# Products of zeros moved into the bank of the weights' sums of squares, each sum made in one run, and a new table of order (block-sparse attention and an MLP, one core of Trainium2)

## The chip, the cores and the metric

The kernel runs on one core of one Trainium2 chip. The metric is the device time of a run in microseconds (us). Below, PE is TensorE, DVE is VectorE, ACT is ScalarE, POOL is GpSimd, and SP is the engine whose queue issues almost all transfers. The kernel before took 716.0 us in the median of 3 runs (714.64 to 716.82).

## The reference, cut to what matters

```python
# batch 4, 8 heads, 768 positions, head dimension 64; blocks of 32 positions, 24 blocks
scores = scale * np.matmul(q, k.transpose(0, 1, 3, 2))
mask = np.abs(blk_i - blk_j) <= 1
mask = mask | (blk_i == 0) | (blk_j == 0) | (blk_i == n_blocks - 1) | (blk_j == n_blocks - 1)
for qb in range(n_blocks):
    for kb in sampled_blocks[qb]:            # 3 random blocks for each block of queries
        mask[qb*32:(qb+1)*32, kb*32:(kb+1)*32] = True
attn = softmax(np.where(mask, scores, -1e9))
x = np.matmul(attn, v)                       # laid out as 3072 tokens x 512
h = x @ w_in                                 # 512 x 2048
g = h * np.tanh(np.log1p(np.exp(h)))
out = g @ w_out                              # 2048 x 512
```

## The kernel before, in words

The work has two halves that share the engines. **Attention** is cut into 52 jobs, 13 for each of the 4 batches (b = 0 to 3, jobs 0 to 12 for b = 0). A job takes two blocks of queries with their sampled keys, or one dense block (the first and the last of a batch). Its steps are the scores on PE (names `s_`, lines 767 for b = 0 and 777 for the others), the maxima on DVE (`mx_`, lines 815 to 820), the exponentials on ACT (`pt_`, line 846), for b = 0 the transposes on PE (`t_`, line 866) with their copies (`pp_`), the products with v on PE (`o_`, lines 931 and 947), the division and the turning of the result on DVE (`xs_`, `tx_`), and its two 16-bit parts (`xh_`, `xl_`). The keys and values of the sampled blocks are gathered by copies on POOL or ACT (`kg`, lines 691 and 693) and by transfers (`vg`, lines 721 to 727).

**The MLP** works on 12 tiles of 256 tokens. Each tile is 16 halves of h (12 matmuls of 128x256 each, line 1206) and 16 pieces of y (6 matmuls of 128x512 each, line 1267). The text calls a half of h or a piece of y a *unit*; there are 384 of them, and they are emitted in a fixed order among themselves. A tile of h needs the outputs of four or five attention jobs. Between h and y, ACT, DVE and POOL form g (`hs`, `us`, `g`, lines 1215 to 1253).

**The weights** arrive as 64-bit numbers and are decoded on DVE by three instructions for each piece (`add_decode`, lines 1059, 1062 and 1065): 8 pieces of w_in (`wr_0` to `wr_7`) and 16 pieces of w_out (`wor_0` to `wor_15`). The sum of squares of the decoded weights gives a power of two as scale: PE multiplies the pieces with themselves into one tile (`gram`, line 468), DVE takes the diagonal of it (line 483), PE adds it up over the partitions (`tp_`), and DVE halves the exponent (`root`, `scales_w`, `scale_o`). w_in has four such scales, each over two pieces, and w_out has one over all 16. Only behind the scale can the weights be split into two 16-bit parts (`wi hi`, `wi lo`, `wo t`, `wo hi`, `wo lo`), which h and y need.

**Products of zeros.** While PE has nothing to do in the first 150 us of the plan, the planner inserts matmuls of a zero tile (line 1038) that nobody reads; they keep PE active. They write into a tile of their own in PSUM: one of the two buffers of ring "h", which are the buffers of h. It is given back when job 9 has begun (`LAST = 9`). So h has one buffer until then.

**What sets the order.** Nothing is issued at once: each step is a task with a planned duration, the engines that can do it, what it reads and writes, and a key from the table `PRIO` (a number for each name and batch). `Plan.emit` then runs a model of the engines forward, always takes the task that can start first (ties by ready time plus key), and emits it. The chip's engines execute in that order, each its own queue, and wait for each other by semaphores. `START` holds planned earliest dates of the first scores, and `RES` a reserve of MLP work. Of the lines that the change touches, these set the shape of the sums of squares:

```python
for n, k in enumerate(keys):
    add("PE", ..., lambda n=n: fn(n), r=[k], w=[kg], new=[(ring, kg)] if n == 0 else (), ...)
```

Each piece of a sum of squares is thus a task of its own, which may stand among other work.

Of the kernel before, what the change touches and what calls it, by code (L numbers as in the profile page):

```python
# [31 lines left out]
    "zrow": (372.5, 343.3, 692.1, -386.3),  # L32
    "zeros": (-1154,),
    "load32 k": (-526.4,),
    "load32 q": (-410.3, -316, 360.9),
    "load v": (-388.9, -306.9, -105.1, -271.1),
    "which": (374.7,),
    "globals": (320.9, 485.3, -720.3, -426.6),
# [18 lines left out]
    "s": (-864, 750.5, -137, 427.9),
    "mx": (410.2, -131.2, 200.2, -747.1),
    "nb": (-606.3, -537, 242),
    "ex": (217.2, -56.8, -191.8, -287.8),  # L60
    "t": (-303.3, 16),
    "pp": (-297.6,),
    "o": (556.5, 15.4, 219, -227.1),
    "xs": (268.3, -141.9, -24.2, -148.8),
    "tx": (-680, -469.1, -691.3, -304.2),
    "xh": (55.5, 554.4, 66.8, 979.6),
    "xl": (-667.3, -368.2, -452.3, -1192),
    "gather k": (622.3, 656.4, 976.5, 1107),
    "gather v": (219.6, 175.4, 18.2, 365.6, -161, 297.2, -517.1, -299.6, -190.2, 611.6, 639.4, 218.3, -570.5,
        -60.5, 269, 108.9, -152.2, 257.3, -154, -170.8, -439.7, -662.4, -12, -183.7, -50.1, 330.5),  # L70
    "load wo": (5.1, 39.8, -463.1, 534.1),
    "decode wor": (-599.6, 24.8, -199.8, -61.5),
    "gram wo": (-838.3,),
    "diag wo": (-562.7,),
    "rootp wo": (178.5,),
    "root wo": (-306.6,),
    "wo t": (-705.8, -195.4, -913.6, -705.3),
    "wo hi": (-316.9, -351.8, -693.9, -792.3),
    "wo lo": (210.8, -523.1, -6.2, 7.7),
    "load k": (59, 59, 59, 134.3),  # L80
    "ss k": (70, 70, 70, 253.6),
    "sc k": (4, 1508, 439.1, 797.7),
    "rootp k": (60, -763.3, 391, -473.3),
    "root k": (7, -270.1, 54.7, -564.5),
    "hi k": (52, -142.1, -699.7, -237.7),
    "lo k": (-79, -88.8, 241.5, 528.5),
    "load q": (59, 59, 59, 665),
    "ss q": (70, 70, 70, -337.7),
    "rootp q": (60, -231.2, -546.9, -273),
    "root q": (7, -533.3, 127.1, -138.6),  # L90
    "hi q": (52, -297.2, -83.6, -744),
    "lo q": (-79, 39.7, -29.6, -293.5),
    "clear": (-985.4,),
    "dense v": (334.4, -79.2, 92.1, -172.8),
    "sc v": (4, 170.2, 343.1, 342),
# [1395 lines left out]
```

## Time and profile before

| what | value |
|---|---|
| median of 3 runs | 716.0 us (714.64 to 716.82) |
| time of the profiled execution | 717.17 us |
| its span in the trace | 715.4 us |
| PE busy | 679.7 us (95%) |
| DVE busy | 579.3 us (81%) |
| ACT busy | 530.6 us (74%) |
| POOL busy | 259.6 us (36%) |

The span is the time from the first to the last event of the trace; what lies around it is 1.8 us. PE counts as busy also while it multiplies zeros or runs at a lower clock, so the share alone does not tell how much of the MLP is done. The first 160 us differ from the rest: there the weights are decoded and PE has less work than time.

### The profile page before, as it was taken

What the parts mean: (1) busy time and instruction counts of PE and PEld (TensorE: products, weight loads), DVE (VectorE), ACT (ScalarE), POOL (GpSimd) and SP (SyncE); (2) the same over time, 40 slices, a digit from 0 to 9 for tenths busy, and PEclk for the clock granted to TensorE, in tenths of its full rate; (3) what the DMA queues carried; (4) which work ended last, traced back from release to release, by engine and by line L of the source; (5) the groups of instructions that cost most, each with busy time, mean ns of one, the idle gap of its engine ahead of it and who ended that gap; (6) DMA issues with size and microseconds to landing.
All of it is one profiled execution on the core that took longest, in us unless ns stands there. A gap on an engine that the chain in (4) does not pass through costs nothing.

```text
span 715.4 us, 25363 instructions
## 1 busy us (share of the span) xinstructions
PE 679.7 (95%) x10349; PEld 451.6 (63%) x10349; DVE 579.3 (81%) x1083; ACT 530.6 (74%) x874; POOL 259.6 (36%) x326
## 2 busy tenths in 40 slices
PE   8877889899999999999999999999999999999997
PEld 3544467666666666666666666666666666666653
DVE  4899999999979977989988978989979868454350
ACT  4845649989888967879878887978798758655440
POOL 3545634874344421544534203533524223000000
PEclk9998999999999999999999999999999999999999
DMA  9978893464785995695656575866655566520000
GB/s 333 383 220 252 269 299 97 124 166 99 173 169 131 199 212 131 163 255 148 143 146 191 137 206 137 245 189 132 162 132 131 134 133 158 131 76 16 16 16 29
DMA packets 144600, 115.94 MB, mean 162 GB/s; under 512 B 96739, under 2 KB 107492, under 8 KB 144484
## 3 DMA queue, kind: packets, MB, share of 16 engines
q1 hardware_dynamic: 144480, 114.33, 60.8%
q8 instruction: 81, 1.33, 0.8%
q14 instruction: 35, 0.29, 0.1%
q10 hardware_dynamic: 4, 0.00, 0.0%
HBM read 79.32 MB, written 12.95 MB: 129 GB/s over the span
## 4 chain that ended last, share of the span: by engine, by line
PE 55%; DVE 25%; ACT 7%; DMA 6%; issue 4%; SPq 1%; POOL 1%; ACTq 0%; POOLq 0%; DVEq 0%
PE y L1267 25%; PE h L1206 22%; PE o L947 3%; PE s L777 3%; DVE mx L820 3%; DMA vg<-vd 2%; ACT pt L846 2%; DVE p L897 2%; DVE wi L1065 2%; DMA wr<-in_moe_w_in_dram 1%; DVE wi L1062 1%; DVE tx L1001 1%; DVE hs L1240 1%; DVE nb L835 1%; DVE xs L978 1%
## 5 line engine op out<-in xcount | busy, mean ns | idle before, releaser
L1206 PE MATMUL h<-xh,wi 128*128 128x256 f16 x1536 | 283.1, 273 | 0.0
L1267 PE MATMUL y<-wo,g 128*128 128x512 f16 x1152 | 277.6, 379 | 1.0 <-ACT ys L1278 0.5
L1206 PEld LDWEIGHTS <-wi 128*128 128x128 f16 x2304 | 222.4, 98 | 58.7 <-issue 4.6
L1206 PE MATMUL h<-xl,wi 128*128 128x256 f16 x768 | 209.8, 273 | 0.0
L1267 PEld LDWEIGHTS <-g 128*128 128x128 f16 x1152 | 109.0, 98 | 104.8 <-issue 5.6
L846 ACT ACTIVATE pt<-s,nb,ns 128x256 f32<-128x256 f32 (+1 forms) x208 | 106.4, 577 | 8.2 <-DVE nb L835 7.3
L691 POOL COPY kg<-kt 128x256 f16 (+1 forms) x147 | 77.3, 564 | 75.0 <-PE s L777 54.8
L1215 ACT ACTIVATE hs<-h 128x512 f32<-128x512 f32 x96 | 56.7, 590 | 60.0 <-PE h L1206 59.8
L1240 DVE SCALAR_TENSOR_TENSOR hs<-us,hs 128x1024 f32<-128x1024 f32 x48 | 64.2, 1337 | 28.0 <-ACT us L1239 28.0
L1021 POOL CAST xh<-tx 128x256 f16<-128x256 f32 (+1 forms) x40 | 28.7, 726 | 121.2 <-DVE tx L1001 120.4
L897 DVE SCALAR_TENSOR_TENSOR p<-pt,p 128x512 f16<-128x512 f32 (+1 forms) x102 | 63.6, 643 | 0.8 <-ACT p L890 0.4
L1230 ACT ACTIVATE us<-hs,hsc 128x1024 f32<-128x1024 f32 x48 | 55.2, 1150 | 1.1
L1234 DVE TENSOR_SCALAR us<-us 128x1024 f32<-128x1024 f32 x48 | 34.1, 711 | 26.8 <-ACT us L1230 26.4
L820 DVE TENSOR_REDUCE mx<-s 128x4 f32<-128x1024 f32 x44 | 53.3, 1212 | 3.0 <-PE s L777 2.2
L1251 POOL TENSOR_TENSOR g<-hs,g 128x1024 f16<-128x1024 f32 x18 | 42.4, 2353 | 34.8 <-DVE g L1248 26.0
L1024 POOL TENSOR_TENSOR xl<-tx,xh 128x256 f16<-128x256 f32 (+1 forms) x45 | 37.5, 838 | 41.7 <-ACT xh L1019 25.8
L1238 ACT ACTIVATE us<-us 128x1024 f32<-128x1024 f32 x48 | 50.7, 1057 | 2.3 <-POOL us L1236 1.3
L1237 ACT ACTIVATE us<-us 128x1024 f32<-128x1024 f32 x38 | 40.1, 1055 | 15.7 <-DVE us L1234 15.6
L1239 ACT ACTIVATE us<-us 128x1024 f32<-128x1024 f32 x48 | 50.7, 1057 | 0.8
L693 ACT ACTIVATE kg<-kt 128x256 f16 (+1 forms) x117 | 36.7, 379 | 13.5 <-DMA kt<-in_k_dram 5.4
L947 PEld LDWEIGHTS <-pp 128*32 128x32 f16 x2952 | 32.5, 97 | 11.9 <-issue 11.4
L1253 DVE TENSOR_TENSOR g<-hs,g 128x1024 f16<-128x1024 f32 x30 | 37.4, 1248 | 2.0 <-ACT g L1246 1.6
(205 smaller groups left out, 914.8 us busy)
## 6 DMA issues: line engine op xcount, KB each, us to landing
vg<-vd SPq DMA_DIRECT2D x304, 65.0 KB, 2.4
vg<-vd SPq DMA_DIRECT2D x80, 195.0 KB, 3.1
wr<-in_moe_w_in_dram SPq DMA_DIRECT2D x8, 1024.0 KB, 10.6
wor<-in_moe_w_out_dram SPq DMA_DIRECT2D x16, 512.0 KB, 6.4
vd<-v SPq DMA_DIRECT2D x12, 520.0 KB, 5.7
raw_v<-in_v_dram SPq DMA_DIRECT2D x12, 512.0 KB, 4.9
out_dram<-ys SPq DMA_DIRECT2D x24, 256.0 KB, 2.4
raw_q<-in_q_dram SPq DMA_DIRECT2D x9, 512.0 KB, 4.8
```

Source lines behind the costliest of these rows:

```text
L691: nc.gpsimd.tensor_copy(out=dst, in_=src)
L820: nc.vector.tensor_reduce(out=mx.rearrange("p g w -> p (g w)"), in_=tl[ks].rearrange("p g (w k) -> p (g w) k", k=KT), axis=AX.X, op=ALU.max)
L846: ex = lambda o, x, g, w: nc.scalar.activation(out=o, in_=x, func=AF.Exp, bias=nb[:, g, w:w + 1], scale=ns(w)[:, 0:1])
L897: nc.vector.scalar_tensor_tensor(out=x[:, 1, cs], in0=src, scalar=PSC, in1=x[:, 0, cs], op0=ALU.mult, op1=ALU.subtract)
L947: nc.tensor.matmul(o[cs, at] if v1 == VW else o[cs, at, 0:v1 - v0], p[:, k, g, cs], x, start=j == 0 and g == 0 and k == 0 and n == 0, stop ...
L1206: nc.tensor.matmul(h[:, f2].rearrange("p (s q) -> p s q", q=BS), wi[:, fp, w, cc, fs], x[:, :, cc], start=f2 == 0 and k == 0, stop=f2 == 1 ...
L1215: nc.scalar.activation(out=tl[kq][:, 2 * (fp % 2):2 * (fp % 2) + 2], in_=tl[kh], func=AF.Copy, scale=-2.0 * GSC)
L1230: nc.scalar.activation(out=us(), in_=hs(), func=AF.Exp, scale=hsc[:, b, k:k + 1])
L1238: add("ACT", 0.97, lambda: nc.scalar.activation(out=us(), in_=us(), func=AF.Ln, bias=1.0), w=[ku], key=K("ln", b))
L1239: add("ACT", 0.97, lambda: nc.scalar.activation(out=us(), in_=us(), func=AF.Exp, scale=-1.0), w=[ku], key=K("un", b))
L1240: add("DVE", 1.15, lambda: nc.vector.scalar_tensor_tensor(out=hs(), in0=us(), scalar=-0.5, in1=hs(), op0=ALU.add, op1=ALU.mult), r=[ku], w ...
L1267: nc.tensor.matmul(tl[ky], tl["g", b, t, k][:, g, f, q], wo[:, fc, w], start=fc == 0 and n == 0, stop=fc == NFC - 1 and n == 2)
```

## The change

Three things change in the code, and a fourth follows from them.

1. The tile into which the products of zeros write is no longer a buffer of h. It is the one buffer of ring "y" (`("yz",)`), which y does not need before w_out is split. It is held until the diagonal of w_out is taken. h has both of its buffers from the start.
2. The sums of squares use the first 128 columns of that same tile, and the products of zeros the other 384, so a product of zeros is 128x384 and no longer 128x512.
3. A sum of squares is one task on PE, which needs all of its pieces: 16 matmuls in a row for two pieces of w_in, 64 in a row for the 16 pieces of w_out.
4. `PRIO`, `START` and `RES` are new in nearly all their numbers, and with them the order of the whole program. The number of products of zeros goes from 119 to 165. The other matmuls keep their number.

```diff
-        for n, k in enumerate(keys):
-            add("PE", 0.8 if key[0] == "wi" else 0.45, lambda n=n: fn(n), r=[k], w=[kg], new=[(ring, kg)] if n == 0 else (),
-                key=K(name, n0), lat=0.25)
+        add("PE", (0.55 if key[0] == "wi" else 0.36) * len(keys), lambda: [fn(n) for n in range(len(keys))],
+            r=[*keys, *([("iv", n) for n in range(NQ)] if key[0] == "wo" else [])], w=[kg], new=[("gy", kg)], use=[("yz",)],
+            key=K(name, n0), lat=0.25)
...
-        add("DVE", 0.4, diag, r=[kg], w=w, new=new_, key=K("diag " + key[0], n0))
+        add("DVE", 0.4, diag, r=[kg], w=w, new=new_, use=[("yz",)], key=K("diag " + key[0], n0))
...
-            nc.tensor.matmul(spare[0].rearrange("p (n q) -> p n q", q=P), z16, z16.unsqueeze(1).to_broadcast([P, 4, P]),
+            nc.tensor.matmul(spare[0][:, P:].rearrange("p (n q) -> p n q", q=P), z16, z16.unsqueeze(1).to_broadcast([P, 3, P]),
...
-    LAST = 9
-    add("PE", 0.0, lambda: spare.append(new(ps["h"], "h", ("zeros",), [P, 512])), w=["zeros"], new=[("h", ("zeros",))],
+    add("PE", 0.0, lambda: spare.append(new(ps["y"], "y", ("yz",), [P, 512])), w=["zeros"], new=[("y", ("yz",))],
...
-        if i == LAST:
-            add("PE", 0.0, spare.clear, r=["zeros", ("begun", i)], use=[("zeros",)], key=K("clear", 0))
...
+            add("PE", 0.0, spare.clear, r=["zeros", ("am", "wo")], use=[("yz",)], key=K("clear", 0))
...
-    RES, START = 949.9, [53.9, 10.3, 0, 62.9, 42.9, 3.5, 60.8, 74.5, 31.2, 92.3, 3.1, 0, 64.4, 30.3, 104.4, 183, 166.3, 159.2]
+    RES, START = 2252, [35.4, 4.3, 15.7, 18.9, 0, 0, 82, 52, 7.4, 64.2, 85.4, 7, 109.7, 96.5, 102.7, 32.5, 161.8, 120]
```

Where the order changes, three places are shown.

**DVE, at the maxima of jobs 8 and 9.** Of before, the rows ahead of the maxima of job 8 (`mx_8`); `wor_7` and `wor_13` are pieces of w_out, and the third instruction of their decoding is L1065:

```order
L1062 SCALAR_TENSOR_TENSOR wo_74<-wor_13_1604,wo_74 128x512
L1065 SCALAR_TENSOR_TENSOR wo_74<-wor_7_1435,wo_74 128x512
L1065 SCALAR_TENSOR_TENSOR wo_74<-wor_13_1604,wo_74 128x512
L968 TENSOR_SCALAR r_5_1719<-o_5_1484,iv_r_117 128x4
L972 RECIPROCAL r_5_1719<-r_5_1719 128x4
L983 TENSOR_TENSOR xs_5_1722<-o_5_1484,r_5_1719 128x256
L820 TENSOR_REDUCE mx_8_1735<-s_8_1538 128x4
```

Of the change, the rows around the maxima of job 9 (`mx_9`), on the same engine:

```order
L1065 SCALAR_TENSOR_TENSOR wo_74<-wor_3_1380,wo_74 128x512
L1059 TENSOR_SCALAR wo_74<-wor_14_1606 128x512
L1065 SCALAR_TENSOR_TENSOR wo_74<-wor_11_931,wo_74 128x512
L1062 SCALAR_TENSOR_TENSOR wo_74<-wor_14_1606,wo_74 128x512
L820 TENSOR_REDUCE mx_9_1749<-s_9_1659 128x4
L1065 SCALAR_TENSOR_TENSOR wo_74<-wor_14_1606,wo_74 128x512
L968 TENSOR_SCALAR r_5_1783<-o_5_1576,iv_r_117 128x4
```

Before, 14 of the 16 pieces of w_out are decoded ahead of the maxima of job 8; now it is 5 of 16, and 10 of 16 ahead of the maxima of job 9. Jobs 8 and 9 stand ahead of decoding that they stood behind.

**DVE, at the end of the decoding of w_out, in the change.** `wor_7` is the last piece, `am_wo` the diagonal of the sum of squares of w_out, and `hs_0_0_0` and `g_0_0_0` belong to the first tile of the MLP:

```order
L1065 SCALAR_TENSOR_TENSOR wo_74<-wor_7_1747,wo_74 128x512
L1001 STREAM_TRANSPOSE tx_6_1981<-xs_6_1962 128x256
L1240 SCALAR_TENSOR_TENSOR hs_0_0_0_1695<-us_0_0_0_1846,hs_0_0_0_1695 128x1024
L1234 TENSOR_SCALAR us_0_0_1_1979<-us_0_0_1_1979 128x1024
L1253 TENSOR_TENSOR g_0_0_0_2055<-hs_0_0_0_1695,g_0_0_0_2055 128x1024
L1240 SCALAR_TENSOR_TENSOR hs_0_0_1_1901<-us_0_0_1_1979,hs_0_0_1_1901 128x1024
L483 SCALAR_TENSOR_TENSOR yz_123,am_wo_2106<-yz_123,ident_64 128x128
```

Before, the diagonal of w_out stands behind the last piece with one such product of the MLP between them (the maxima of job 9 and the first part of one g besides); now two groups of h are that far ahead of it.

**PE, at the end of the run of w_out, in the change.** The last of the 64 matmuls into `yz_123` stand between the two halves of `h_0_0_4`, the fifth group of h of the first tile:

```order
L468 MATMUL yz_123<-wo_74 128x128
L931 MATMUL o_7_2063<-vg0_114,pp_7_0_1635 32x65 x16
L1206 LDWEIGHTS wi_73
L1206 MATMUL h_0_0_4_1965<-xh_0_0_599,wi_73 128x256
L1206 LDWEIGHTS wi_73
L1206 MATMUL h_0_0_4_1965<-xl_0_0_600,wi_73 128x256
```

Of before, a piece of the same sum (`gram_wo_1389`), which stands between the two halves of the first group of h; 11 more pieces follow, among h, scores and products with v:

```order
L1206 MATMUL h_0_0_0_1624<-xh_0_0_560,wi_73 128x256
L468 LDWEIGHTS wo_74
L468 MATMUL gram_wo_1389<-wo_74 128x128
L468 LDWEIGHTS wo_74
L468 MATMUL gram_wo_1389<-wo_74 128x128
```

So nine units of h stand ahead of the run, and the run ahead of everything else. When PE comes to the scores of job 13 (`s_13`, the first of batch 1), it has 32 units behind it in the change (26 halves of h and 6 pieces of y), and 27 before (22 and 5). The attention steps ahead of `s_13` on PE are the same in both.

## Rows read from the trace of the kernel before

**Rows 1.** Busy time by stretch: us, then PE, PEld, DVE, ACT, POOL, clock.

```profile
core 0: us, PE busy (x) PEld busy (x) DVE busy (x) ACT busy (x) POOL busy (x), PEclk, DMA share, GB/s
...
80.00:100.00 20.00, 16.44 (x228) 10.76 (x228) 18.44 (x37) 10.23 (x17) 7.59 (x8) 0.91 0.91 300
...
120.00:150.00 30.00, 28.12 (x532) 20.50 (x531) 29.49 (x47) 29.78 (x44) 25.25 (x27) 0.94 0.48 126
...
200.00:300.00 100.00, 98.62 (x1584) 66.58 (x1583) 87.31 (x183) 80.96 (x135) 39.54 (x47) 1.00 0.72 169
```

**Rows 2.** PE in order of time: start, us, work.

```profile
89.76 0.28 PE L1206 MATMUL h<-xh,wi 128*128 128x256 f16 x1
...
98.60 0.63 PE L468 MATMUL gram_wo<-wo 128*128 128x128 bf16 x8 [1.16 <-DVE wo L1065]
...
107.31 0.60 PE L866 MATMUL t<-ident,pt 128*128 128x128 f32 x4
...
110.86 0.39 PE L468 MATMUL gram_wo<-wo 128*128 128x128 bf16 x4
...
150.83 0.66 PE L931 MATMUL o<-vg,pp 128*32 128x65 f32 x32
...
159.06 1.17 PE L777 MATMUL s<-kt,q 64*32 64x512 f16 x48
```

**Rows 3.** The chain that ended last: one half of h, one piece of y.

```profile
161.63 1.31 PE h L1206 x12
...
173.60 1.30 PE y L1267 x6
```

**Rows 4.** DVE in order of time, at five places.

```profile
57.23 3.04 DVE L1065 SCALAR_TENSOR_TENSOR wi<-wr,wi 128x1024 int32<-128x1024 int32 x1
...
61.73 0.27 DVE L483 SCALAR_TENSOR_TENSOR gram_wi<-gram_wi,ident 128x128 f32<-128x128 f32 x1
...
107.72 1.47 DVE L1065 SCALAR_TENSOR_TENSOR wo<-wor,wo 128x512 int32<-128x512 int32 x2
...
110.25 1.21 DVE L820 TENSOR_REDUCE mx<-s 128x4 f32<-128x1024 f32 x1
...
160.99 1.21 DVE L815 TENSOR_REDUCE mx<-s 128x2 f32<-128x1024 f32 x1
```

**Rows 5.** Groups by line and shape: count, busy us, mean ns.

```profile
L1240 DVE SCALAR_TENSOR_TENSOR hs<-us,hs 128x1024 f32<-128x1024 f32 x48 | 64.2, 1337 | 28.0 <-ACT us L1239 28.0
...
L1065 DVE SCALAR_TENSOR_TENSOR wo<-wor,wo 128x512 int32<-128x512 int32 x16 | 11.0, 703 | 0.0
...
L1062 DVE SCALAR_TENSOR_TENSOR wo<-wor,wo 128x512 int32<-128x512 int32 x16 | 12.2, 770 | 0.0
...
L1059 DVE TENSOR_SCALAR wo<-wor 128x512 int32<-128x512 int32 x16 | 8.3, 532 | 1.3 <-DMA wor<-in_moe_w_out_dram 1.3
...
L1253 DVE TENSOR_TENSOR g<-hs,g 128x1024 f16<-128x1024 f32 x30 | 37.4, 1248 | 2.0 <-ACT g L1246 1.6
...
L1248 DVE CAST g<-hs 128x1024 f16<-128x1024 f32 x30 | 21.1, 704 | 9.1 <-PE y L1267 8.8
...
L1024 DVE TENSOR_TENSOR xl<-tx,xh 128x128 f16<-128x128 f32 x5 | 3.5, 726 | 0.0
...
L879 DVE COPY pp<-t 128x512 f32<-128x512 f32 x10 | 6.8, 676 | 1.2 <-PE t L866 1.2
...
L835 DVE TENSOR_SCALAR nb<-mx,ns 128x4 f32<-128x4 f32 x16 | 9.4, 588 | 0.1
...
L1230 ACT ACTIVATE us<-hs,hsc 128x1024 f32<-128x1024 f32 x48 | 55.2, 1150 | 1.1
...
L693 ACT ACTIVATE kg<-kt 128x256 f16 x87 | 29.6, 407 | 2.3 <-PE s L777 1.3 <-POOL kg L691 0.5 <-DVE us L1234 0.3
```

**Rows 6.** PE and its clock while h already ran.

```profile
101.00:104.00 3.00, 3.00 (x47) 0.50 1.10 349
...
138.50:141.50 3.00, 2.92 (x42) 0.50 0.24 62
```

More of the change, by code (lines that the diff above doesn't have):

```diff
@@ L27 @@
              xs=1, hs=3, us=3, g=4, ys=1, kt=1, q=2, ssk=2, ssv=2, ssq=2, sck=2, scv=2, scq=2, iv=2, ns=3, ws=2,
-             wq=2, am=2, p16=3, tx=1)
+             wq=2, am=2, gy=1, p16=3, tx=1)
 PRIO = {
[L32 to L38, printed above, removed]
[16 rows of a table removed]
-    "gsc": (-69.1,),
-    "open": (163,),
@@ L57 @@
[L57 to L95, printed above, removed]
-    "ends": (13, 542.7, 466.1, 1080),
-    "hi v": (52, -74.3, 62.8, 85.1),
@@ L111 @@
-    "un": (184.5, 575.9, -457.3, -178.2),
-    "hm": (-41.7, 485.8, 146.2, 619.7),
-    "gh": (91.4, 381.2, 177, -262.4),
-    "gl": (259.1, 389.1, 749.5, 495.9),
-    "ys": (-27.1, -7.7, -30.1, -83.4),
-    "out": (-436.7, -87.9, 351.5, -286.7),
+    "zrow": (35.9, 246.1, 437.6, -570.6),
+    "zeros": (-488.9,),
+    "load32 k": (-802.2,),
+    "load32 q": (-960.9, -534.7, 391.8),
+    "load v": (-780, -345.7, -304.5, 138.6),
+    "which": (466.7,),
+    "globals": (142.5, -437.7, -1403, -1272),
[16 rows of a table added]
@@ new lines @@
+    "gsc": (300.2,),
+    "open": (389.4,),
+    "s": (-293.5, 1022, 204.8, 611.3),
+    "mx": (660.3, -204.8, 662.9, -265.1),
+    "nb": (-619.9, -926.8, -586, 120.7),
+    "ex": (990.9, -35, -144.6, -626.4),
+    "t": (-84.8, 16),
+    "pp": (-432.7,),
+    "o": (165.9, -309.5, 166.2, -1448),
+    "xs": (423.7, -118.7, 436.6, -211.1),
+    "tx": (-1314, -228.9, -1034, -842.6),
+    "xh": (336.7, 776.3, -829.3, 987),
+    "xl": (-360, 272, -807.1, -1820),
+    "gather k": (1627, 1242, 1408, 1924),
@@ new lines @@
+    "gather v": (-99.1, 229.5, -365.9, 124.5, -1214, 89.8, -418.7, -635.6, -870.5, 52.6, 605.1, -399.6, -812.7,
+        -990.2, -232.3, -274.4, 114.7, 465.5, 322.4, -311.2, -865.1, -1403, -12, 41.5, -164.9, -935.3),
+    "load wo": (-794.8, 65.7, -849.6, -124.7),
+    "decode wor": (110.5, 349.6, 151.2, 6.4),
+    "gram wo": (-630.1,),
+    "diag wo": (-474.9,),
+    "rootp wo": (814,),
+    "root wo": (76.4,),
+    "wo t": (-666.7, -198.5, -869.3, -544.1),
+    "wo hi": (-500.6, -568.5, -2019, -1351),
@@ new lines @@
+    "wo lo": (907.4, 209, -229.4, 528),
+    "load k": (59, 59, 59, 109.7),
+    "ss k": (70, 70, 70, 502.5),
+    "sc k": (4, 1966, 411.7, 478.6),
+    "rootp k": (60, -467.2, 366.9, 94.8),
+    "root k": (7, -600.5, -43.8, 76.4),
+    "hi k": (52, -339.8, -523.1, -983.6),
+    "lo k": (-79, -183.7, 30, 930.6),
+    "load q": (59, 59, 59, 1108),
+    "ss q": (70, 70, 70, -492.2),
+    "rootp q": (60, -28.9, -566, -296.9),
+    "root q": (7, 800.5, 1558, 177.1),
+    "hi q": (52, -1543, -55.5, -1201),
@@ new lines @@
+    "lo q": (-79, 890.5, 13.8, 697.8),
+    "clear": (-533.4,),
+    "dense v": (491.3, 238.7, 144.2, 44.6),
+    "sc v": (4, 927.9, 58.3, 736.4),
+    "ends": (13, 423.4, -397.3, 921.3),
+    "hi v": (52, 100.3, 279.8, 729.5),
+    "lo v": (-79, 546, 1023, 944.8),
+    "hsc": (-435.9, 330.5, -730, 644.6),
+    "osc": (295, -1852, -6.5, -52.9),
+    "h16": (17, 860.2, -243.8, 1145),
+    "l16": (-40, 31.6, -504.4, 352.2),
+    "tdma": (-60, 484.1, 236.1, 332.1),
+    "xc": (1, 149.8, 2067, 1365),
@@ L238, in emit @@
             if t.eng == "PE" and self.zeros and self.FROM < start < self.TILL and idle > 0.25:
-                self.zeros(int((idle - 0.3) / (0.25 if start > 15.0 else 0.4)))
+                self.zeros(int((idle - 0.3) / (0.2 if start > 15.0 else 0.33)))
             for e in t.ways:
```

27 lines of the change are left out of this document (13 added, 14 removed), and 32 rows, old and new, of the table PRIO.

## The prediction

> **What bounds the kernel now.** The forecast is **712.7 us**, 3.3 us below the median of before. I read the busy time by stretch first, because a share over the whole span mixes two regimes here. From 200 to 300 us PE is busy 98.62 of 100 us at full clock [rows 1], and the chain that ends last runs through h and y without a gap, one unit each 1.31 or 1.30 us [rows 3]. There the end is set by the amount of PE work that is left, and nothing else. Ahead of that it is otherwise: from 80 to 100 us DVE is busy 18.44 of 20 us and PE 16.44, a part of that with zeros and at a clock of 0.91; from 120 to 150 us ACT is busy 29.78 of 30 us and DVE 29.49, and PE still has 1.88 us without work [rows 1]. So DVE (decoding, maxima), then ACT, set when the attention steps come; PE fills up with units of h and y. From about 150 us PE is the bound.
>
> The scores of job 13, at 159.06 us [rows 2], are a good fence between the two. The time is (date of these scores) + (PE work behind them). A unit done ahead of them is 1.31 us that need not be done behind; each us by which they come later is a us lost. Both kernels have the same attention steps ahead of them on PE, so two numbers decide: how many units stand ahead, and how late the scores come.
>
> **Units ahead of the scores of job 13.** The order has 32 in the change and 27 before: 5 x 1.31 = **6.5 us** less work behind them. They fit in because h has two buffers from the start. Before, one was held by the zeros till job 9 had begun, so the second group of h had to wait for the first to be read. Behind job 13 the order keeps a lead of 5 to 7 units up to job 24 and gives it back until the end (all 384 units are done in both); that is harmless while PE has no gap.
>
> **Date of the scores of job 13.** Three routes lead to it; each is costed by itself.
>
> *DVE.* I summed the instructions that stand ahead of the maxima of job 13, which on DVE began at 160.99 us [rows 4], each with the mean of its form. The change puts ahead of them 2 of L1240 (2 x 1.337 us), 2 of L1248 (2 x 0.704) and two parts of `wi` (0.70 + 1.25 us, my sum from the forms with like shapes, L1248 and L1253); it takes away 2 of L1024 (2 x 0.726), 2 of L879 (2 x 0.676) and 2 of L835 (2 x 0.588) [rows 5]. That is 6.0 - 4.0 = +2.0 us. To this comes one stall. The last decoding of w_in ended at 57.23 + 3.04 = 60.27 us and its diagonal began at 61.73 [rows 4]; the 1.46 us between, in which PE squares the last piece, held the division and the turning of job 2. In the change the diagonal stands right behind the decoding, so about 1.3 us of it become idle time, on an engine that has none to spare. Together **+3.3 us**.
>
> *ACT.* 16 instructions of decoding that stood ahead of the maxima of job 9 now stand behind them: 5 x 0.532 + 5 x 0.770 + 6 x 0.703 = 10.7 us [rows 5], and with others that move along, these maxima come some 13 us or more earlier than 110.25 us [rows 4]. But ACT has 37 instructions more between the exponentials of job 9 and of job 13, parts of `us` at 1.150 us and copies of keys at 0.407 us [rows 5] among them: about 17 us. What is won at job 9 is spent by job 13: 17 - 13 to 17 - 16, **+1 to +4 us**.
>
> *PE.* The first h began at 89.76 us [rows 2]; what it waits for (w_in's parts, the first tile's input) comes about as before. Nine units (11.8 us), one step of scores (1.17) and some products with v and transposes (0.6 to 0.66 each) [rows 2, 3] bring PE to the run of w_out at about 106 us. The last decoding began its pair at 107.72 and ended at 109.2 us [rows 4]; by the same list of DVE it ends at 109.8, and with the stall at 111.1 us. So **PE waits some 4 us in the run**, in front of a queue that holds everything: the products with v of job 7, the rest of h, the scores of job 10. 28 of the 64 matmuls lie ahead of `wor_7` and go during the wait; the 36 of it and behind it take 36 x 79 to 98 ns (0.63 us for 8, 0.39 for 4 [rows 2]), 2.8 to 3.5 us, so PE is free at about 114.2. Then come 23 units (30.1 us), 11 halves of products with v (6.6), 7 steps of transposes (3.9), 3 of scores (4.0), small sums and changes of work (about 2): 160.8 us if nothing waits. With the 1.88 us that PE idled from 120 to 150 us [rows 1] it is 162.7; with one more stretch of 3 us at a clock of 0.50, as two stand in the trace of before [rows 6], half of it is lost, 1.5 us: 164.2. Against 159.06 that is **+1.7 to +5.1 us**, +3.6 at the waits of before.
>
> All three lie near +3.3, so I take 162.4 us.
>
> **Edits that I cost at nothing.** Zeros: 165 of 384 columns for 119 of 512 (0.418 us in the page's mean, overlapped) are 4% more columns; they stand where PE waits. The run itself adds no matmul. The wait of 4 us replaces waits like the 1.16 us ahead of a piece at 98.60 [rows 2], and its price is in PE's route. `clear` and the ring "y" free the tile with the diagonal of w_out; y needs w_out split behind that anyway. Behind job 13 DVE (87.31 of 100) and ACT (80.96) have room [rows 1], so a changed order there hides behind PE's units; if that cover fails, PE's share of 98.62 in such a stretch falls, 1 us for each per cent.
>
> **The shared tile.** Before, zeros and sums had tiles of their own, so PE could multiply zeros while DVE took a diagonal. Now `diag` and the zeros use one tile, and the order has zeros behind a run wait for DVE. The diagonal of w_in began 1.46 us behind the decoding [rows 4]: a few such gaps of 1 to 2.5 us, up to four, are 0 in the sum while DVE sets the pace there (18.44 of 20 us [rows 1]), and 4 x 2.5 = 10 us of PE without zeros if not; their harm would be a lower clock for the first units, up to 1.5 us by a stretch like [rows 6].
> The Trainium skill, "PSUM — Partial Sum Buffer", section "PSUM bank collisions raise a hardware error", says that two engines must not access one bank and quadrant at once, even in different columns. It speaks against this change, since separate columns do not free PE from waiting; the order agrees with it, and no run so far shows the price.
>
> **Sum.** -6.5 + 3.3 = -3.2 to -3.3 us. On the profiled execution (717.17 us, of it 715.4 span) this gives 713.9; it lies 1.2 us above the median of the runs, on which I put the forecast: 716.0 - 3.3 = 712.7 us.
>
> **Rivals.**
> - *The lead is kept in full*: the scores of job 13 come no later, since DVE's stall is filled and the work that is put ahead replaces idle time. 716.0 - 6.5 = 709.5 us. DVE at 18.44 of 20 us [rows 1] speaks against it. Chance 0.15.
> - *The change does not do what the counts say*: the lead is taken back, by the scores at +5.1 (714.6) or by new gaps of 2 to 3 us behind job 13, where order is new throughout and one unit less lies between the last h and its y. About 716 us, 714 to 718. Chance 0.27.
> - *The run of w_out stalls PE longer* (the slower side). Its place is the wait ahead of the last pieces: every us by which the decoding of `wor_7` ends later than 111.1 is a us of PE, with nothing to do beside it, while before only 4 matmuls waited there and h went on. It decides for slower when the scores come later than 159.06 + 6.5 + 2.15 = 167.7 us, that is when the last piece ends behind about 116 us. For it: decoding is spread among more work of jobs 8 and 9 and the MLP. Against it: by DVE's list it is as early as before to 2 us. At 10 us late: about 721 us. Chance 0.12.
> - *The shared tile starves PE of zeros*, so units run at a clock of 0.50: 3 us of units at half clock lose 1.5 us, and four of them more would be needed for 718.7. Chance 0.04.
>
> **How the numbers follow.** 0.3% of 716 us, 2.15 us, is about what a measurement can tell from no change. My forecast (710.5 to 713.85) has 0.42; with the full lead's 0.15, faster has 0.57. No change has 0.27 and slower 0.16. The likeliest case alone reaches from -6.5 + 1.7 (711.2) to -6.5 + 5.1 (714.6). The range for 8 in 10 takes in the full lead, 709.3, and the larger part of no change, up to 717.5.
>
> **What would show it.** Right: h runs in both buffers from its first group; PE idles 3 to 5 us in front of the last pieces of the run, near 107 to 111 us; an idle of about 1.3 us stands ahead of one diagonal of w_in on DVE; the scores of job 13 come at 161 to 164 us; 200 to 300 us stays at 98 to 99 busy. Wrong: scores of job 13 behind 167 us, PE under 97 in a stretch behind them, or a clock below 0.8 for the first tiles.

## The result, and the profile after

The change took **723.05 us** in the median of 4 runs (721.11 to 725.33), the kernel before 715.47 beside it: ratio 1.0108 [1.0075, 1.0140]. It is slower by 1.1%, and the forecast of 712.7 us (709.3 to 717.5) was wrong. The profiled execution of the change was the fastest of its four, 721.11 us with a span of 719.3; that of before lay above its median. So the two traces differ by only 3.9 us where the medians differ by 7.6. The change was profiled once more among the experiments (e16), in an execution above its median (726.84 us).

The frame of the prediction holds: time is the date of the scores of job 13 plus the work behind them. Behind them are 719.3 - 170.80 = 548.5 us now and 715.4 - 159.06 = 556.3 before, 7.8 less (forecast: 6.5). The scores come 11.7 us later (forecast: 3.3). The second trace of the change, e16, against the same trace of before, gives +15.1 and -5.4; the mean of both, +13.4 - 6.6 = +6.8, is near the difference of the medians. Everything that went wrong lies ahead of the scores of job 13.

Busy time by stretch of the change (us, length, then PE, PEld, DVE, ACT, POOL, clock, DMA), for [rows 1]:

```profile
core 0: us, PE busy (x) PEld busy (x) DVE busy (x) ACT busy (x) POOL busy (x), PEclk, DMA share, GB/s
0.00:170.80 170.80, 143.87 (x2373) 102.72 (x2373) 144.67 (x256) 114.67 (x209) 82.51 (x106) 0.92 0.72 222
...
80.00:100.00 20.00, 16.06 (x327) 12.36 (x327) 17.86 (x33) 11.41 (x30) 9.08 (x10) 0.83 0.81 255
...
120.00:140.00 20.00, 17.39 (x266) 12.54 (x267) 18.35 (x46) 17.77 (x28) 11.46 (x13) 1.00 0.34 87
...
200.00:300.00 100.00, 98.93 (x1625) 66.44 (x1624) 85.53 (x177) 85.34 (x152) 34.52 (x41) 1.00 0.69 168
```

The same view of the kernel before, up to its scores of job 13:

```profile
0.00:159.06 159.06, 134.30 (x2274) 89.80 (x2274) 143.13 (x257) 108.25 (x196) 87.09 (x110) 0.94 0.78 241
```

DVE has 144.67 - 143.13 = 1.5 us more work up to the fence; its time without work went from 15.9 to 26.1 us. From 200 to 300 us nothing is lost.

PE of the change in order of time (start, us, work, in brackets the idle time ahead and what ended it), for [rows 2]:

```profile
83.00 1.96 PE L931 MATMUL o<-vg,pp 128*32 128x65 f32 x64 [3.86 <-issue]
...
90.63 0.28 PE L1206 MATMUL h<-xh,wi 128*128 128x256 f16 x1
...
110.59 3.83 PE L468 MATMUL yz<-wo 128*128 128x128 bf16 x64
...
117.28 0.38 PE L494 MATMUL tp_q<-ss_q,ones 128*128 128x1 f32 x2 [0.85 <-ACT pp L877]
...
120.73 0.38 PE L494 MATMUL tp_wo<-am_wo,ones 128*128 128x1 f32 x2 [1.06 <-DVE pp L879]
...
130.53 0.27 PE L1206 MATMUL h<-xh,wi 128*128 128x256 f16 x1 [1.33 <-POOL xh L1021]
...
131.35 0.27 PE L1206 MATMUL h<-xl,wi 128*128 128x256 f16 x1 [0.55 <-POOL xl L1024]
...
146.14 0.66 PE L931 MATMUL o<-vg,pp 128*32 128x65 f32 x32 [0.49 <-DVE pp L879]
...
150.49 1.09 PE L931 MATMUL o<-vg,pp 128*32 128x65 f32 x32 [3.10 <-DVE pp L879]
...
164.15 1.00 PE L866 MATMUL t<-ident,pt 128*128 128x128 f32 x4 [0.71 <-ACT pt L846]
...
170.80 1.17 PE L777 MATMUL s<-kt,q 64*32 64x512 f16 x48
```

The run of w_out is free at 114.42 us, where the forecast had 114.2; but PE came to it at 110.59 us instead of at about 106 and did not wait in it. The delay took the place of the forecast wait of 4 us, so that this date was right by luck, and in this execution alone: in e16 the last piece ends at 113.93 us and the run at 119.22.

```profile
113.25 0.68 DVE L1065 SCALAR_TENSOR_TENSOR wo<-wor,wo 128x512 int32<-128x512 int32 x1
```

```profile
115.39 3.83 PE L468 MATMUL yz<-wo 128*128 128x128 bf16 x64
```

Behind the run come seven waits, 8.1 us together, for steps on three engines (ACT, DVE and POOL). The longest, 3.10 us, is for a copy on DVE (`pp`, line 879); in e16 it is 3.10 us again.

DVE of the change, for [rows 4]:

```profile
82.02 0.21 DVE L968 TENSOR_SCALAR r<-o,iv_r 128x4 f32<-128x4 f32 x1
82.48 0.42 DVE L983 TENSOR_TENSOR xs<-o,r 128x256 f32<-128x256 f32 x1
...
110.16 0.68 DVE L1065 SCALAR_TENSOR_TENSOR wo<-wor,wo 128x512 int32<-128x512 int32 x1
...
116.78 1.22 DVE L1240 SCALAR_TENSOR_TENSOR hs<-us,hs 128x1024 f32<-128x1024 f32 x1 [1.83 <-ACT us L1239]
117.92 0.29 DVE L483 SCALAR_TENSOR_TENSOR yz<-yz,ident 128x128 f32<-128x128 f32 x1
...
122.67 0.23 DVE L1147 TENSOR_SCALAR scq<-gsc,sc_o 128x4 f32<-128x4 f32 x1
...
172.85 1.24 DVE L815 TENSOR_REDUCE mx<-s 128x2 f32<-128x1024 f32 x1
```

What stands on DVE ahead of that copy, in the change and then in the kernel before:

```profile
146.01 2.19 DVE L835 TENSOR_SCALAR nb<-mx,ns 128x4 f32<-128x4 f32 x1
148.12 1.72 DVE L1234 TENSOR_SCALAR us<-us 128x1024 f32<-128x1024 f32 x1
149.76 1.27 DVE L879 COPY pp<-t 128x512 f32<-128x512 f32 x2
```

```profile
137.08 0.25 DVE L835 TENSOR_SCALAR nb<-mx,ns 128x4 f32<-128x4 f32 x1
137.24 0.68 DVE L1234 TENSOR_SCALAR us<-us 128x1024 f32<-128x1024 f32 x1
137.84 0.68 DVE L879 COPY pp<-t 128x512 f32<-128x512 f32 x1
```

The two instructions ahead of it took (2.19 - 0.25) + (1.72 - 0.68) = 3.0 us longer, about the whole wait. Beside the first, POOL had one instruction (line 1251) from 146.04 to 148.17 us, beside the second another (line 1163). The first took 2.18 to 2.20 us in all twelve traces with the new order at this place (the change, e1 to e4, e6, e7, e9, e11, e13, e16, e18). PE waited 2.9 to 3.1 us in the seven where the second took 1.72 us, and 1.9 to 2.1 us in the five where it did not. That POOL held DVE up is argued from these dates; no run moves one of the two.

The last piece is decoded at 110.84 us (forecast: 111.1). The diagonal of w_out, which the order puts behind two groups of h, comes at 117.92, and the scale (`scq`) at 122.67, 12 us behind the last piece. This late scale was my first suspect: theory A in the expectations. Theory B there is the order, which makes the engines wait for each other; C is the zeros in the shared tile, D the tile and the runs in any order, H a hold of job 10.

### The profile page after: what moved, and what is told of

It reads as the page before. It is cut to its first block, busy times and chain, and to the rows that moved or that the text cites. A ratio compares the mean times of both kernels' runs of the same rounds, so it can differ in the third digit from the quotient of the medians.

```text
span 719.3 us, 25462 instructions
## 1 busy us (share of the span) xinstructions
PE 682.7 (95%) x10395; PEld 459.4 (64%) x10395; DVE 562.1 (78%) x1079; ACT 538.8 (75%) x896; POOL 233.1 (32%) x308
## 4 chain that ended last, share of the span: by engine, by line
PE 52%; DVE 20%; ACT 13%; DMA 8%; issue 4%; POOL 1%; SPq 1%; ACTq 0%; POOLq 0%; DVEq 0%
PE y L1267 23%; PE h L1206 21%; PE o L947 3%; PE s L777 3%; DMA vg<-vd 3%; ACT pt L846 3%; DMA raw_q<-in_q_dram 2%; DVE hs L1240 2%; DVE mx L820 2%; DMA wr<-in_moe_w_in_dram 2%; ACT us L1238 1%; DVE p L897 1%; ACT hs L1215 1%; DVE us L1234 1%; ACT us L1237 1%
## 5 line engine op out<-in xcount | busy, mean ns | idle before, releaser
L691 POOL COPY kg<-kt 128x256 f16 (+1 forms) x120 | 57.1, 514 | 144.4 <-PE s L777 116.7
L1240 DVE SCALAR_TENSOR_TENSOR hs<-us,hs 128x1024 f32<-128x1024 f32 x48 | 59.6, 1243 | 36.8 <-ACT us L1239 36.7
L897 DVE SCALAR_TENSOR_TENSOR p<-pt,p 128x512 f16<-128x512 f32 (+1 forms) x102 | 65.5, 660 | 3.0 <-ACT p L890 2.5
L693 ACT ACTIVATE kg<-kt 128x256 f16 (+1 forms) x144 | 45.1, 380 | 17.0 <-DMA kt<-in_k_dram 6.7
L1251 POOL TENSOR_TENSOR g<-hs,g 128x1024 f16<-128x1024 f32 x16 | 37.3, 2328 | 54.8 <-ACT g L1246 34.7
L1021 POOL CAST xh<-tx 128x256 f16<-128x256 f32 (+1 forms) x44 | 24.5, 565 | 85.2 <-DVE tx L1001 73.7
L1234 DVE TENSOR_SCALAR us<-us 128x1024 f32<-128x1024 f32 x48 | 36.4, 758 | 13.4 <-ACT us L1230 13.3
L1253 DVE TENSOR_TENSOR g<-hs,g 128x1024 f16<-128x1024 f32 x32 | 39.4, 1231 | 1.1 <-ACT g L1246 0.7
```

The source lines that it names most:

```text
L691: nc.gpsimd.tensor_copy(out=dst, in_=src)
L897: nc.vector.scalar_tensor_tensor(out=x[:, 1, cs], in0=src, scalar=PSC, in1=x[:, 0, cs], op0=ALU.mult, op1=ALU.subtract)
L1240: add("DVE", 1.15, lambda: nc.vector.scalar_tensor_tensor(out=hs(), in0=us(), scalar=-0.5, in1=hs(), op0=ALU.add, op1=ALU.mult), r=[ku], w ...
```

## The experiments

All kernels but e7 and e8, which leave out a part of h, compute what the change computes; they differ in what is emitted when. For that the emitted list is recorded and rearranged, or replaced by a list written out:

```diff
-            fn()
+            rec.append((t, fn))
...
+        [fn() for _, fn in arrange(rec)]
```

**e1: the diagonal of w_out earlier on DVE**, behind `g_0_0_0` and ahead of `hs_0_0_1`.

```diff
+    put(rec, ("am", "wo"), ("g", 0, 0, 0), "DVE")
```

> The changed kernel (723.05 us median, before 715.47) with one instruction moved on DVE: the diagonal of w_out stands ahead of the second hs of the first tile, which had waited 1.83 us for ACT, instead of behind it. Theory A (the loss is the late scale of w_out: it comes at 122.5 us instead of 113.7, because the sum of squares is one run of 64 products and the diagonal stands behind a stalled product): the scale comes 2 to 3 us earlier and the time falls by 2 to 3 us, to 720 or 721. Theory B (the new order makes PE, DVE and ACT wait for each other from 110 to 170 us, wherever the scale comes): within 1 us of 723.

726.17 us, ratio 1.0125 [1.0083, 1.0167]. The diagonal now stood and waited 2.13 us for the run, which PE reached only at 117.96 us, and the scale came at 127.85 us, 12.4 us behind the last piece. So this edit did not make the scale early and does not try theory A. The scores of job 13 came at 175.1. No gain; the time lies above both ranges.

**e2: the run of w_out in 16 pieces**, each behind its own decoding, still in the shared tile.

```diff
+    run = rec.pop(at(rec, ("gram", "wo")))[0]
+    for n, (s, fc) in reversed(list(enumerate(spots))):
+        rec.insert(s, (run, lambda n=n, fc=fc: piece(fc, n == 0, n == 15)))
```

> The changed kernel with the run of 64 products of w_out cut up again: each piece stands on PE where it has been decoded (six of them in one run right behind the last products of zeros, since these share the bank), all else in the order of the change. Theory A: the sum ends some 2 us earlier, 1 to 2 us gained if DVE takes it up, 721 to 722. Theory B: within 1 us of 723, since the diagonal stands where it stood. The range of a rival, that the run itself costs PE 3.8 us which the pieces hide in waits: 719 to 720.

726.46 us, 1.0135 [1.0102, 1.0168], above all three ranges; scores of job 13 at 171.7. Cutting the run up gains nothing in this order.

**e3: e2 with the diagonal, its sum and the scale early.**

```diff
+    put(rec, ("am", "wo"), ("us", 0, 0, 1), "DVE", 0, 1)
+    put(rec, ("tp", "wo"), ("h", 0, 0, 4), "PE", 0, 1)
+    put(rec, "sc_o", ("tp", "wo"))
+    put(rec, ("hs", 0, 0, 1), "sc_o")
```

> As the kernel with separate pieces, and the whole way from the last piece to the scale of w_out put ahead as it was before the change: diagonal right behind the decoding, the copy that its sum over partitions waits for ahead of two of ACT's exponentials, the sum and the scale ahead of the second hs. The scale should come at 114 to 116 us instead of 122.5. Theory A: most of the 7.6 us come back, 715 to 718. Theory B: at most 2 us come back, 721 to 723, and the scores of job 13 stay behind 168 us.

722.99 us, 1.0110 [1.0075, 1.0145]. DVE of this kernel, and the scores of job 13 on PE:

```profile
111.54 0.68 DVE L1065 SCALAR_TENSOR_TENSOR wo<-wor,wo 128x512 int32<-128x512 int32 x1
...
117.46 0.23 DVE L1147 TENSOR_SCALAR scq<-gsc,sc_o 128x4 f32<-128x4 f32 x1
```

```profile
170.50 1.17 PE L777 MATMUL s<-kt,q 64*32 64x512 f16 x48
```

The scale stands 5.2 us behind the last piece instead of 12, and the scores come as late as ever. PE had a new wait of 2.16 us at 124.27 us, for the sums of squares of the keys of batch 1. In this execution the first h came at 93.45 us, and from there to the scores of job 13 it is 77.1 us, against 80.2 and 79.7 in the two traces of the change; the median shows no such gain. As the whole of the loss, theory A falls.

**e4: the change without products of zeros.**

```diff
+def arrange(rec):
+    return [x for x in rec if x[0] is not None]
```

> The changed kernel without any products of zeros (165 matmuls that nobody reads are left out; nothing else moves). Theory C (the shared tile: zeros wait for the diagonals and hold PE up in the first 90 us): PE comes earlier to its work, the time falls by 1 to 3 us. Theories A and B: the zeros stand in idle time and only keep the clock up; without them the first scores, products and units run at 0.50, and the time rises by 1 to 6 us, 724 to 729.

727.42 us, 1.0143 [1.0111, 1.0175]. Its first 90 us:

```profile
0.00:90.00 90.00, 49.27 (x1022) 35.52 (x1027) 73.48 (x132) 46.20 (x96) 40.60 (x60) 0.72 0.80 266
```

PE is busy 49.27 us there, in the change 73.67 at a clock of 0.87. Taking all zeros away does not help. The lower clock could hide a gain, but PE's dates show none: it comes to the products with v of job 4 at 84.42 us and to the first h at 93.84, in the change at 83.00 and 90.63 (e16: 85.83 and 94.45). So zeros that wait in the shared tile are not what holds PE up. Theory C falls.

**e5 and e6: code and order apart.** e5 has the change's code in the order of before (each run at the place of its last piece); e6 has the code of before in the new order, with its own tiles for the sums, but each sum in one run. `ORDER` is the recorded list of the other kernel, task by task with its engine.

```diff
+ORDER = """
...
+"""
+def arrange(plan):
+    return [plan.tasks[int(x[1:])].ways[eng[x[0]]][1] for x in ORDER.split()]
```

> The changed code in the order of the kernel before: every task on every engine stands where it stood before the change (written out as a list), and only the edits 1 to 3 are in it: zeros of 384 columns in the bank of y (119 of them), h with two buffers from the start, each sum of squares in one run at the place of its last piece. Theory B (the order alone costs the time): as before, 714 to 718, scores of job 13 at 158 to 161 us. Theory D (the shared bank and the runs cost it in any order): 719 to 724.

> The code of before in the order of the change: zeros of 512 columns in a buffer of h (165 of them, given back ahead of the second group of h), the sums of squares in tiles of their own, but each in one run as the order has it. Theory B: as the changed kernel, 721 to 727, scores of job 13 at 169 to 173 us. Theory D: 715 to 719.

e5: 717.76 us, 1.0028 [1.0003, 1.0054]. e6: 722.95 us, 1.0081 [1.0050, 1.0112]. e5 on DVE and PE:

```profile
113.49 0.30 DVE L483 SCALAR_TENSOR_TENSOR yz<-yz,ident 128x128 f32<-128x128 f32 x1 [3.29 <-PE yz L468]
```

```profile
160.38 1.17 PE L777 MATMUL s<-kt,q 64*32 64x512 f16 x48
```

The order carries most of the loss. Tile, runs and the second buffer of h together cost about 0.28%, 2 us, an interval that only just leaves out zero. The place where that could arise in e5 is the 3.29 us in which DVE waits for the run on PE; no run takes this wait away.

**e7 and e8: five units less ahead of job 13**, in the change and in the kernel before. Five halves of the first tile are cut to one product each; the rest of them is left out.

```diff
-            prods = [(w, x, cc) for cc in range(NCC) for w, x in ((0, xh), (0, xl), (1, xh))]
+            prods = [(w, x, cc) for cc in range(NCC) for w, x in ((0, xh), (0, xl), (1, xh))][:1 if (b, t) == (0, 0) and 10 <= 2 * fp + f2 <= 14 else None]
```

> The changed kernel with five halves of h cut short, the tenth to the fifteenth unit but one, which stand between the run of w_out and the scores of job 10: one product instead of twelve in each (this part of h is left out; all reads and all else stay), 6.0 us of PE less ahead of job 10. If PE's own work sets the date of the scores of job 13, as the sum of PE's route has it, they come 5 to 6.5 us earlier (164 to 166) and the time falls by 5 to 6.5 us, to 717 to 719. If DVE or ACT sets the pace there (the routes that the prediction summed up), PE idles in the place of the units: 0 to 2.5 us earlier, and the end comes 0 to 2.5 us earlier.

> The kernel before with the same five halves of h cut short to one product each (this part of h is left out), 6.0 us of PE less, between 113 and 122 us. If DVE sets the pace there (19.38 of 20 us busy from 100 to 120 us), the scores of job 13 come 0 to 2 us earlier than 159.06 and the time falls by as little, since PE only idles; if PE's work sets it, 5 to 6.5 us earlier and 709 to 711 us.

e7: 723.55 us, 1.0103 [1.0063, 1.0144]; e8: 717.23 us, 1.0013 [0.9983, 1.0043]. e7 from 120 to 140 us:

```profile
120.00:140.00 20.00, 13.63 (x176) 8.23 (x175) 17.55 (x40) 17.75 (x29) 7.93 (x11) 0.74 0.38 103
```

6 us of PE work taken out gave no time back: in e7 the scores come at 173.0. In e8's trace they come at 156.21, 2.9 us earlier than before, and its median shows no gain. PE is not what sets the pace there; in e7 it only stood still more and ran at a lower clock (0.74 against 1.00).

**e9 to e12: one order up to a seam, the other behind it.** Seams: the first h (e9 old first, e10 new first) and the scores of job 10 (e11 old first, e12 new first). The edit is the list alone, as in e5.

> The changed code with two orders put together: up to the first h (about 90 us) every engine follows the order of before, behind it the order of the change (what is left, in its sequence). Theory P (the new order loses the time in the first 90 us: in all runs of it the third maxima come at 49 to 50 us instead of 45, and the decoding of w_out ends at 111 to 115 instead of 106 to 109): as the changed code in the old order or a little above, 716 to 719. Theory Q (it loses it between the first h and the scores of job 13, where units, the scale of w_out and the keys of batch 1 stand): as the change, 721 to 726.

> The other way about: the new order up to the first h, behind it the order of before (27 units ahead of the scores of job 13 again). Theory P: 720 to 725. Theory Q: 716 to 719, scores of job 13 at 159 to 163 us.

> The changed code, the order of before up to the scores of job 10, the new order behind them; since s_10 is the first task of the second part and the new order has five more units ahead of it, those come ahead of it here too. If the loss lies ahead of job 10 (first h to s_10): 715 to 719. If it lies between job 10 and job 13: 720 to 724. If the five units ahead of s_10 hold it by themselves: s_10 at 128 to 131 us and 719 to 722.

> The new order up to the scores of job 10, the order of before behind them. If the loss lies ahead of job 10: scores of job 10 at 132 to 137 us, scores of job 13 at 166 to 172, and the time 720 to 727, or more, since the 5 units of lead are spent again by the old order (27 units ahead of job 13). If it lies behind job 10: 715 to 719.

| kernel | us | ratio | scores of job 13 | behind them |
|---|---|---|---|---|
| e9 | 721.48 | 1.0073 [1.0055, 1.0090] | 172.6 | 548.3 |
| e10 | 732.71 | 1.0214 [1.0187, 1.0240] | 175.1 | 557.9 |
| e11 | 723.20 | 1.0100 [1.0069, 1.0130] | 172.6 | 549.8 |
| e12 | 725.94 | 1.0148 [1.0124, 1.0172] | 167.9 | 555.2 |

By its expectation e9 speaks for theory Q: most of the loss lies behind the first h. The first 90 us of the new order cost some 0.34% (1.0107 [1.0086, 1.0128] for the change run again, below, against 1.0073 [1.0055, 1.0090]; the intervals touch). The others say little of the change, since a seam makes waits of its own, and e10 lies above both of its ranges; e10 on PE:

```profile
112.20 1.96 PE L931 MATMUL o<-vg,pp 128*32 128x65 f32 x64 [10.71 <-DMA raw_q<-in_q_dram]
```

**e13 and e14: the scores of job 10 earlier.** From the maxima of job 10 to those of job 13 it is 35 to 38 us in the traces up to here (e12 aside, which has 32), and those of job 10 come at 135.78 us in the change and at 125.27 before. So a hold of job 10 could be the whole delay. e13 moves the scores of job 10 and what they need ahead in the change; e14 takes the old order up to the exponentials of job 10. Both edits are in the list alone.

> The changed kernel with job 10 ahead of its hold: the scale of q of batch 1 directly behind that of k on DVE, the scores of job 10 on PE behind the products of job 8 with v (14 units ahead of them, not 17, and no h of the second tile), their maxima and exponentials some places earlier on DVE and ACT. Nothing else moves, the scores of job 13 keep 32 units ahead. Theory H (a hold on job 10): its scores at 126 to 129 us instead of 132.6, those of job 13 at 164 to 167, the time 4 to 6 us below the change. Theory U (the units ahead, with their work on ACT and DVE, fill the time whatever the place of job 10): scores of job 13 at 169 to 172, within 2 us of the change.

> The changed code, the order of before up to and with the scores, maxima and exponentials of job 10, the new order behind them (the run before of this kind left job 10 to the new order, and had 723.2 us, scores of job 13 at 172.6). Theory H: maxima of job 10 at 125 to 128, scores of job 13 at 162 to 165, time 711 to 714, since 32 units are ahead of them. Theory U: scores of job 13 at 168 to 172, time 717 to 721.

e13: 728.15 us, 1.0166 [1.0146, 1.0185], its maxima of job 10 at 133.3 us. e14: 727.25 us, 1.0139 [1.0118, 1.0160], maxima at 124.4. Job 13 in e13:

```profile
178.72 1.17 PE L777 MATMUL s<-kt,q 64*32 64x512 f16 x48
```

e13 brought job 10 only 2.5 us forward, less than was expected; e14 is the better trial. Job 10 came earlier and job 13 later, here and in e14 (175.5), and both times lie above both of their ranges. Theory H falls.

**e15 and e16: the old order with the new order's units ahead of job 13, and the change again.** e15 goes up to the scores of job 13 in the old order, with five units more ahead of them.

> The changed code in the order of before up to the scores of job 13, the new order behind, which puts its five more units directly ahead of those scores (32 in all). Their 6.5 us come at a place where nothing else is held but job 13: scores of job 13 at 160 + 6.5 = 166 to 168, work behind them as in the change (548 to 550), time 715 to 718: neither gained nor lost against the changed code in the old order (717.8).

> The changed kernel as it is, once more, on the same chip as the three others, to compare them with: 721 to 727 us, scores of job 13 at 170 to 174.

e15: 720.64 us, 1.0043 [1.0022, 1.0064]. e16: 724.90 us, 1.0107 [1.0086, 1.0128]. e15 on PE:

```profile
166.80 1.17 PE L777 MATMUL s<-kt,q 64*32 64x512 f16 x48
```

That is 6.4 us behind e5 (160.38), and 5 x 1.31 = 6.5 us is what five units take. So at this place they delayed the scores by their whole time, and behind them gave back about half of it (551.8 against 555.1 us in e5, 3.3 of 6.4 in these two executions). The time missed the expected 715 to 718 us; the intervals of e15 and e5 overlap.

**e17 and e18: the two places by themselves.** In the change, PE stands idle ahead of the products with v of job 4. The idle time is 2.9 to 6.4 us in the traces of the change's order up to there. These products write the one buffer of ring "o" and need the division of job 3 to have read it, and on DVE that stands behind some 10 us of work, most of it decoding of w_out. e17 moves it ahead of that, word for word on DVE:

```diff
 L1062 SCALAR_TENSOR_TENSOR wo<-wor_909,wo 128x512
+L968 TENSOR_SCALAR r_1348<-o_1190,iv_r 128x4
+L972 RECIPROCAL r_1348<-r_1348 128x4
+L983 TENSOR_TENSOR xs_1351<-o_1190,r_1348 128x256
 L1062 SCALAR_TENSOR_TENSOR wo<-wor_918,wo 128x512
...
 L1174 TENSOR_SCALAR gsc<-iv_i,rg 128x4
-L968 TENSOR_SCALAR r_1390<-o_1190,iv_r 128x4
-L972 RECIPROCAL r_1390<-r_1390 128x4
-L983 TENSOR_TENSOR xs_1393<-o_1190,r_1390 128x256
```

e18 is e9 with the diagonal and the scale of w_out early, to try the late scale once more behind an old start:

```diff
 L1234 TENSOR_SCALAR us_0_1_1933<-us_0_1_1933 128x1024
+L483 SCALAR_TENSOR_TENSOR yz,am_wo<-yz,ident 128x128
 L1253 TENSOR_TENSOR g_0_0_2009<-hs_0_0_1680,g_0_0_2009 128x1024
-L1240 SCALAR_TENSOR_TENSOR hs_0_1_1856<-us_0_1_1933,hs_0_1_1856 128x1024
-L483 SCALAR_TENSOR_TENSOR yz,am_wo<-yz,ident 128x128
```

> The changed kernel with one group of three instructions moved on DVE: the division of job 3, which had waited behind some ten us of decoding (its sum stood ready in the only buffer o from 74.5 us on, and was divided at 84.9 us; PE idled 3.9 to 6.4 us in front of the products of job 4 with v in every run of the new order), stands 17 tasks earlier. If that division is the first place: products of job 4 at 80 to 82 us instead of 83 to 87, first h at 90 instead of 92 to 95, 721 to 723 us. If not: within 1 us of 724.9.

> The order of before up to the first h and the new one behind (721.5 us), with the diagonal and the scale of w_out put ahead as in the kernel with separate pieces and early scale (the run of 64 stays). If the late scale is the second place: scale at 116 to 118 instead of 123.4, scores of job 13 at 167 to 169 instead of 172.6, 717.5 to 719.5 us. If the five units with their work are it: within 1 us of 721.5.

e17: 721.92 us, 1.0059 [1.0038, 1.0079]. Its trace is of an execution of 732.61 us, so it shows where the moved instructions stand and cannot show what they gained. e16 (the change again) on PE and on DVE:

```profile
85.83 1.96 PE L931 MATMUL o<-vg,pp 128*32 128x65 f32 x64 [5.59 <-issue]
```

```profile
84.85 0.21 DVE L968 TENSOR_SCALAR r<-o,iv_r 128x4 f32<-128x4 f32 x1
85.31 0.42 DVE L983 TENSOR_TENSOR xs<-o,r 128x256 f32<-128x256 f32 x1
```

e17, the same two engines:

```profile
81.07 0.66 PE L931 MATMUL o<-vg,pp 128*32 128x65 f32 x32
```

```profile
76.76 0.21 DVE L968 TENSOR_SCALAR r<-o,iv_r 128x4 f32<-128x4 f32 x1
77.21 0.42 DVE L983 TENSOR_TENSOR xs<-o,r 128x256 f32<-128x256 f32 x1
```

The row on PE says "issue", which names nobody. DVE's rows do: the division ends at 85.31 + 0.42 = 85.73 us and the products begin at 85.83; in the first profile of the change 82.90 and 83.00. With the division moved, the products come 4.8 us earlier than in e16, and the ratio falls from 1.0107 to 1.0059, with intervals that do not overlap (that of the first result, from 1.0075 on, touches the 1.0079 at which e17's ends). So the wait is shown, and that it costs time. The way from it to the end is not: in the trace of e17, PE then stands 4.25 us for ACT's exponentials, and the first h comes at 96.70 us instead of the expected 90.

e18: 724.43 us, 1.0086 [1.0061, 1.0111], no better than e9. Its scale came at 119.73 us and its diagonal had waited 2.72 us for the run; the scores of job 13 came at 174.1. The expectation missed either way, and the late scale is again not it.

No kernel here beat the one before.

## Why the prediction was wrong

**The frame and the units were right.** 32 and 27 units stand ahead of job 13; behind it 547.6 to 551.8 us are left in the traces with 32 units (e17 aside), 555 to 558 with 27. The reason given for it was wrong. "They fit in because h has two buffers from the start": in the program of before the second group of h waits for PE's own zeros, not for a reader, and its trace has no such wait.

**The failed step is the date of the scores of job 13, in its waiting times.** On DVE the work was right (+1.5 us for +2.0), but "one stall", about 1.3 us, is +10.2 us of waiting. On PE, "PE waits some 4 us in the run" was wrong: PE reached the run at 110.59 us (e16: 115.39), not at about 106, and in neither trace did it wait there. The 64 matmuls in a row took 3.83 us, 60 ns each, where the prediction had 79 to 98. That the last piece and the end of the run were right to 0.3 us in the first trace is luck, as told above. Behind the run, "with the 1.88 us that PE idled" was 8.1 us: 114.42 + 48.3 of work + 8.1 = 170.8, where the prediction had 114.2 + 46.6 + 1.9 = 162.7. In e16 it is 119.22 + 48.16 + 6.76 = 174.14: there the run is 5.0 us late, and the waits are 4.9 us longer. I had summed each engine's list in its new order and kept the waits of the old one. Such a sum is a lower bound: it holds only if the other two engines deliver in time, and they had new orders too.

**What stands in its place**, in shares of the loss of 1.07 to 1.08%. Each share is a difference of two medians and uncertain by about 0.3%:
- *Tile and runs, about 0.28%* (e5). "The run itself adds no matmul" was true and not enough: the diagonal of a scale can now wait for a run that PE reaches late (3.29 us in e5, 2.13 in e1, 2.72 in e18). In the change itself it did not wait, so how the share arises there is not shown.
- *The order up to the first h, about 0.34%* (e16 against e9). That "what it waits for (w_in's parts, the first tile's input) comes about as before" was wrong: the first h came at 92.3 to 96.1 us in the other traces of the change's order up to it, against 89.76; the change's first profile, 90.63, was the best of them. One cause is the division of job 3 behind decoding (e17); that it is the whole of this share is not shown. DVE also waited for pieces of the weights there, which the prediction had not counted: in e16 for 1.11 us at 56.44, 1.47 at 80.25 and 1.78 at 90.58, in the first profile and in before for none between 55 and 90 us.
- *The order from the first h on, about 0.45%* (e9 against e5), what the five units gave back behind job 13 included. The late scale (e3, e18), the hold of job 10 (e13, e14) and the five units (e15) were each tried and none is it alone. What the traces show is seven waits of 0.5 to 3.1 us on PE, for ACT, DVE and POOL in turn; in e3 an early scale brought a new one. The longest stands behind two instructions of DVE that took 3.0 us longer beside POOL's, where the prediction had "each with the mean of its form". Which edges of the order make the others stays open, and no run tried what the longest is worth.

**The gain.** The five units ahead were to fill idle time. In e15 they pay their whole time ahead of the fence; PE's idle from the first h to job 13 was 6.4 us before and 10.4 in the change, so it was not filled but grew. The first rival, the lead kept in full, needed it filled.

**The slower rival** had the right threshold, 167.7 us, and the wrong place: PE did not wait in the run. The last piece ended at 110.84 us, in e16 at 113.93, both ahead of its mark of 116. It had 0.12, all slower cases 0.16: too little for an order that was new throughout, which the prediction named only as "new gaps" within no change.

**The shared tile.** The diagonal of w_in waited 0.73 us instead of 1.3, and the run without zeros (e4) was no faster. The Trainium skill, "PSUM — Partial Sum Buffer", section "PSUM bank collisions raise a hardware error", says that two engines must not use one bank and quadrant at once even in different columns. e5's cost agrees in sign, but it holds the runs too. e6 keeps the runs and has tiles of their own for zeros and sums: 1.0081 against 1.0107 for the change, 0.26% with intervals that overlap, so no price of the shared bank is shown.

**Behind job 13** all was as forecast: PE 98.93 of 100 us busy from 200 to 300 us.

## What to carry to other kernels

When an order is new on every engine, the sum of an engine's own list is only the lower bound of a date; for each ring of one buffer look up where, in the queue of the engine that frees it, the freeing instruction now stands, and what is ahead of it. Work put ahead of a fence costs its time there unless the trace shows idle time at that very place, and taking work away from an engine that others hold up gives little back (e7, e8). A wait whose row says "issue" can still be a full buffer: compare its end with the end of the last reader on the other engines. The mean time of an instruction hides the places where it takes longer: here 2.19 us against 0.25 made most of the longest wait.
